# Attention and a feed-forward block in one kernel: heads split over the two row halves, scores over two banks, and the last eight units in one list

## The chip, the cores and the metric

The kernel runs on one core of one Trainium2 chip. The metric is the device time of one execution in microseconds (us). The profile used here is one execution, taken by the hardware profiler. Its engines are PE (TensorE, matrix products; PEld is its weight loads), DVE (VectorE), ACT (ScalarE), POOL (GpSimd) and SP (SyncE, which only issues DMA transfers here).

## The reference

Inputs are q, k, v of 4 batches x 8 heads x 768 tokens x 64 channels, 8 memory keys and values for each batch and head, and a feed-forward block of width 512 to 2048 and back. Attention goes by chunks of 32 queries; each chunk sees the 8 memory rows, 16 tokens to the left, its own 32 and 8 to the right, 64 rows in all.

```python
for c in range(nc):
    ...
    k_full = np.concatenate([mem_k, k_ctx], axis=2)
    v_full = np.concatenate([mem_v, v_ctx], axis=2)
    scores = scale * np.matmul(q_c, k_full.transpose(0, 1, 3, 2))
    scores = scores - np.max(scores, axis=-1, keepdims=True)
    a = np.exp(scores)
    a = a / (np.sum(a, axis=-1, keepdims=True) + 1e-09)
    out[:, :, c_start:c_end] = np.matmul(a, v_full)
...
xn = (x - mu) / np.sqrt(var + 1e-06) * g_ln
ch = np.maximum(xn @ w_ch1, 0.0) @ w_ch2
return (x + ch).astype(np.float32)
```

## The kernel before, in words

**Tiles and units.** The 3072 tokens are 24 tiles t of 128 tokens, six to a batch; t and t+1 form a unit u of 256 tokens, so there are 12 units. A tile passes through these steps:

- `qk_products` (line 311): 32 products of 32 queries x 64 keys, scores of 8 heads and 4 chunks, into one PSUM bank.
- `row_max`, `less_max` on DVE, `weights` (exp) on ACT, `pt_products` (four transposes on PE) and `pt_copy`.
- `val_products` (line 366): 32 products of 32 queries x 65 columns (64 channels and a column of ones that sums the weights) into the two banks of `two`.
- `tokens` on DVE divides by the sums and takes the mean, `shift` (ACT or POOL) subtracts it, `square` and `root_of` make the reciprocal deviation, `x_products` and `x_copy` turn the tile for the feed-forward block.

A unit then has eight `up_products` (two blocks of 128 hidden channels each, eight products of 128x256), each followed by `relu_up`, and seven `down7_products` of eight products each, the seven-product scheme of a 2x2 block product, with sums `r_sum` on DVE before and `add_to` on DVE behind. Units 10 and 11 go up in the seven-product scheme as well (`up7_products`, `hold`, `relu_of_sum`, `relu_sum`), whose weight sums are `w1_sum` and `x_sum`.

**Where operands lie.** Keys and queries are loaded as rows of 8 tokens (`load_octets`), interleaved by a copy (`mix`), turned by PE (`turn_whole`, called by `later_k` and `later_q`) and copied to KT (`to_stream`) and QD (`to_rows`). Of a pair of heads j, the even head lies on partitions 0 to 63 and the odd one on 64 to 127. The values lie in V: for each group of two chunks, chunk 0 of all heads on partitions 0 to 63 and chunk 1 on 64 to 127, with memory rows copied in by `v_mem` and the rows that both chunks see copied by `v_shared` (SBUF to SBUF, issued by SP). `load_v_head` and `load_v_ends` load V for batches 2 and 3.

**Positions in the array.** A product names its place by `tile_position`, a row half (0 or 64) and a column quarter (0, 32, 64, 96). Scores before use (0, 0), (64, 32), (0, 64), (64, 96), values the same four.

**PSUM.** Eight banks of 128x512: `one` (two, lent out in turn by `slot()`), `two` (two banks, for values), `upb` (two) and `dnb` (two).

**What sets the order.** Scheduling is manual: each engine runs its instructions in the order of the text, and waits on semaphores where data or banks are missing. Units 0 to 2 and 8 to 11 are written out call by call. Units 3 to 7 come from a plan: for each unit, 16 steps alternate `up` and `down7` of the unit before, and `at(u, step, ...)` places the rest. In it `val` of a tile and `qk` of the tile two later stand at one step, values first. A DMA issued by SP or POOL stands in that engine's queue like any other instruction.

Of the kernel before, what the change touches and what calls it, by code (L numbers as in the profile page):

```python
# [9 lines left out]
FP32 = mybir.dt.float32  # L10
# [8 lines left out]
def kernel(  # L19
# [33 lines left out]
    last = sb.tile([128, 1], FP16, name="last")  # L53
    w1c = [sb.tile([128, 4, 512], FP16, name=f"w1c{i}") for i in range(4)]
# [26 lines left out]
    one = [ps.tile([128, 512], FP32, name=f"one{i}") for i in range(2)]  # L81
# [29 lines left out]

    def load_v_head(b, h, part):

        base = (b * H + h) * HS
        if part == 0:
            nc.gpsimd.dma_start(  # L116
                out=V[b % 2][72:128, 0 : NG - 1, h, 0:64],
                in_=dram(v, base + 16 * D, [[64, 56], [64 * 64, NG - 1], [1, 64]]),
            )
        else:  # L120
            nc.gpsimd.dma_start(
                out=V[b % 2][0:32, 1:NG, h, 0:64],
                in_=dram(v, base + 48 * D, [[64, 32], [64 * 64, NG - 1], [1, 64]]),
            )

    def load_v_ends(b):
        nc.gpsimd.dma_start(
            out=V[b % 2][72:120, NG - 1, :, 0:64],
            in_=dram(v, b * H * HS + (64 * (NG - 1) + 16) * D, [[64, 48], [HS, H], [1, 64]]),
        )  # L130
        nc.gpsimd.dma_start(
            out=V[b % 2][16:32, 0, :, 0:64],
            in_=dram(v, b * H * HS, [[64, 16], [HS, H], [1, 64]]),
        )
# [131 lines left out]
    def mix(i, half, engine):  # L266
        for jj in range(2):
            mix_into(mixed[i], raw[i][half], jj, 96, engine)
# [41 lines left out]

    def qk_products(t, p=None):
        b, tt = t // 6, t % 6
        p = slot() if p is None else p
# [16 lines left out]
    def row_max(t, scores):  # L330
        nc.vector.tensor_reduce(out=nmx[t % 2], in_=scores, axis=AX.X, op=ALU.max)

    def less_max(t, scores):
        nc.vector.tensor_tensor(  # L334
            out=sub[t % 2].rearrange("p (c k) -> p c k", c=8), in0=scores,
            in1=free(nmx[t % 2], 0, [[1, 8], [0, 64]]), op=ALU.subtract,
        )
# [28 lines left out]
    def val_products(t):  # L366
        b, tt = t // 6, t % 6
        for h in range(H):
# [670 lines left out]
    mix(0, 0, "P")  # L1039
# [52 lines left out]

    plan = {}
# [6 lines left out]
    for u in range(3, NP - 4):  # L1100
# [12 lines left out]
    for b in range(2, B):  # L1113
        u0 = 3 * b - 3
        for half in range(2):
            w = u0 - 1 + half
            if w > 2:
                at(w, 1, load_octets, 0, half, k, b, 48 * half, 48)
                at(w, 3, load_octets, 1, half, q, b, 48 * half, 48)
                at(w, 12, mix, 0, half, "V")  # L1120
            at(w + 1, 5, mix, 1, half, "A")
            for n, step in enumerate((1, 6, 11, 15)):
                if n < 2:
                    at(w + 1, step, later_k, b, half, n, "V")
                else:
                    at(w + 1, step, later_q, b, half, n - 2, "A")
            for n in range(8):
                if w > 2:
                    step = (0, 2, 4, 12, 13, 14, 15, 16)[n]
                    at(w, step, load_v_head, b, 4 * half + n // 2, n % 2)  # L1130
                else:
                    at(4, n // 2, load_v_head, b, n // 2, n % 2)
        at(u0 + 1, 0, load_v_ends, b)
        at(u0 + 1, 10 if b == 2 else 6, v_shared, b, 0, NG)
        if b == 2:
            at(3, 8, v_mem, b)
        else:
            at(u0 + 1, 6, v_mem, b)
        at(u0, 14, mem_cols, KT[b % 2], memT[:, 4 * b : 4 * b + 4, :])
        at(u0, 14, mem_ends, KT[b % 2], memT[:, 4 * b : 4 * b + 4, :])  # L1140

    for u in range(2, NP - 5):
        for m, step in ((0, 0), (1, 1), (2, 3), (3, 5)):
            plan.setdefault((u + 1, step), []).insert(0, (r_sum, (u, m)))

    for u in range(3, NP - 4):
# [9 lines left out]

    r_sum(7, 0)
    up_products(8, 3, one[1])
    relu_up(8, 3, one[1], "A")
    val_products(18)  # L1160
    tokens(18)
    r_sum(7, 1)
    s20 = qk_products(20, upb[0])
    row_max(20, s20)
    up_products(8, 1, upb[1])
    w1_sum(2, 0, 1, "P")
    relu_up(8, 1, upb[1], "A")
    square(18)
    root_of(18)
    w1_sum(2, 0, 0, "P")  # L1170
    down7_products(7, 0, dnb[0])
    w1_sum(0, 0, 1, "P")
    down7_products(7, 1, dnb[1])
    add_to(14, 0, dnb[0])
    val_products(19)
    s21 = qk_products(21, one[0])
    less_max(20, s20)
    shift(18, "A")
    s22 = qk_products(22, one[1])
    w1_sum(0, 1, 1, "P")  # L1180
    up_products(8, 4, upb[1])
    w1_sum(0, 0, 0, "V")
    row_max(22, s22)
    weights(20)
    less_max(22, s22)
    weights(22)
    down7_products(7, 2, dnb[0])
    row_max(21, s21)
    add_to(14, 0, dnb[1])
    less_max(21, s21)  # L1190
    tokens(19)
    up_products(8, 0, upb[0])
    up_products(8, 5, one[1])
    relu_up(8, 4, upb[1], "A")
    relu_up(8, 5, one[1], "A")
    p20 = pt_products(20, dnb[1])
    pt_copy(20, p20, "A")
    x18 = x_products(18, upb[1])
    weights(21)
    r_sum(7, 2)  # L1200
    shift(19, "P")
    up_products(8, 6, one[0])
    down7_products(7, 3, one[1])
    square(19)
    p21 = pt_products(21, dnb[1])
    add_to(14, 1, dnb[0])
    add_to(15, 1, one[1])
    relu_up(8, 0, upb[0], "A")
    pt_copy(21, p21, "A")
    val_products(20)  # L1210
    tokens(20)
    relu_up(8, 6, one[0], "A")
    w1_sum(2, 1, 0, "P")
    down7_products(7, 4, dnb[0])
    add_to(15, 1, dnb[0])
    up_products(8, 7, upb[0])
    val_products(21)
    s23 = qk_products(23, dnb[1])
    r_sum(7, 3)
    x_copy(18, x18, "A")  # L1220
    tokens(21)
    relu_up(8, 7, upb[0], "A")
    up_products(8, 2, one[0])
    down7_products(7, 6, dnb[0])
    row_max(23, s23)
    less_max(23, s23)
    x19 = x_products(19, upb[1])
    relu_up(8, 2, one[0], "A")
    r_sum(8, 2)
    x_copy(19, x19, "A")  # L1230
    weights(23)
    shift(20, "P")
    r_sum(8, 0)
    down7_products(8, 1, upb[0])
    add_to(15, 0, dnb[0])
    w1_sum(1, 0, 0, "P")
    w1_sum(3, 0, 0, "P")
    shift(21, "P")
    down7_products(8, 0, one[0])
    add_to(16, 0, one[0])  # L1240
    r_sum(8, 1)
    p22 = pt_products(22, dnb[1])
    pt_copy(22, p22, "A")
    x21 = x_products(21, upb[1])
    down7_products(7, 5, one[1])
    val_products(22)
    x_copy(21, x21, "A")
    root_of(19)
    up_products(9, 3, dnb[0])
    relu_up(9, 3, dnb[0], "A")  # L1250
    up_products(9, 0, dnb[1])
    w1_sum(1, 0, 1, "P")
    square(20)
    square(21)
    w1_sum(0, 1, 0, "V")
    add_to(14, 1, one[1])
    store(14)
    tokens(22)
    shift(22, "P")
    p23 = pt_products(23, upb[1])  # L1260
    pt_copy(23, p23, "V")
    down7_products(8, 2, one[0])
    add_to(16, 0, upb[0])
    x20 = x_products(20, one[1])
    x_copy(20, x20, "A")
    add_to(16, 1, one[0])
    val_products(23)
    tokens(23)
    down7_products(8, 3, dnb[0])
    add_to(17, 1, dnb[0])  # L1270
    shift(23, "P")
    down7_products(8, 4, one[0])
    up_products(9, 2, upb[1])
    x22 = x_products(22, upb[0])
    add_to(17, 1, one[0])
    down7_products(8, 6, one[0])
    w1_sum(1, 1, 1, "V")
    x_copy(22, x22, "V")
    w1_sum(3, 1, 1, "P")
    x23 = x_products(23, one[1])  # L1280
    x_copy(23, x23, "V")
    x_sum(0, "V")
    x_sum(1, "P")
    x_sum(3, "P")
    relu_up(9, 0, dnb[1], "A")
    up_products(9, 1, dnb[1])
    up_products(9, 4, upb[0])
    relu_up(9, 4, upb[0], "A")
    w1_sum(3, 0, 1, "P")
    relu_up(9, 1, dnb[1], "A")  # L1290
    add_to(17, 0, one[0])
    store(17)
    up7_products(0, 1, one[1], False)
    r_sum(8, 3)
    hold(one[1], held[0][0])
    up_products(9, 7, one[0])
    relu_up(9, 7, one[0], "V")
    up7_products(0, 2, upb[0], False)
    up7_products(1, 1, dnb[1], False)
    hold(dnb[1], held[1][0])  # L1300
    down7_products(8, 5, dnb[0])
    add_to(16, 1, dnb[0])
    up_products(9, 6, one[0])
    relu_of_sum(0, 0, 0, upb[0], held[0][0])
    up7_products(0, 6, one[1], True)
    hold(one[1], held[0][1])
    up7_products(1, 6, dnb[1], True)
    hold(dnb[1], held[1][1])
    up7_products(1, 2, dnb[0], False)
# [160 lines left out]
```

## Time and profile before

| what | us |
|---|---|
| median of 3 runs (lowest, highest) | 224.51 (224.37, 224.60) |
| the profiled execution | 224.37 |
| its span, first to last instruction on the core | 222.7 |
| ACT busy | 132.8 |
| POOL busy | 133.9 |
| relu of the up products, ACT, one of 128x512 | 0.60 |
| add of a down product, DVE, one of 128x256 | 0.48 |
| transpose of a batch's keys or queries on PE, start to start | 0.345 |

The span leaves out 1.7 us around the first and last instruction. In a timeline a row gives start, duration, engine, line, operation, operands (written <- read) and how many were merged. A product's duration is its way through the array (0.27 us for 256 columns); products overlap, so what one costs is the distance between starts. In the answers by windows a row gives the stretch, its length, then busy time and count for each engine, the granted clock as a share of full speed, the busy share of the 16 DMA engines and GB/s. The granted clock is 1.0 in the whole span.

### The profile page before, as it was taken

The page shows a single profiled execution, that of the slowest core. Times are in us where ns is not written, and L with a number is a line of the kernel's source. Part 1 is how long each engine was busy: PE and PEld are TensorE (multiplying, and loading weights), DVE is VectorE, ACT ScalarE, POOL GpSimd, SP SyncE. Part 2 cuts the span into 40 slices and gives each one's busy share as a digit, 9 for nine tenths or more (in the row PEclk, how much of TensorE's full clock was granted, in tenths as well). Part 3 has the DMA queues.
Part 4 walks back from the last instruction along what each step waited for, and adds up shares of the span by engine and source line. Part 5 has one row for each costly group of instructions (what it writes and reads, how often), then busy time and mean ns, then how long its engine had stood idle before and what let it go on. Part 6 is the DMA issues. An engine that isn't in the chain of part 4 may idle for free.

```text
span 222.7 us, 8325 instructions
## 1 busy us (share of the span) xinstructions
PE 213.0 (96%) x3581; PEld 187.1 (84%) x3581; DVE 175.6 (79%) x388; ACT 132.8 (60%) x262; POOL 133.9 (60%) x210
## 2 busy tenths in 40 slices
PE   6986999999899999999999999999999999999993
PEld 2455877789888989999999999999898999999982
DVE  1587767888889887896686996995789987788983
ACT  3298875886775388468447278378757743654100
POOL 7948399989879617966454937415277548830000
PEclk9999999999999999999999999999999999999999
DMA  5999999999979993994952992952100011101115
GB/s 75 192 199 203 214 211 208 138 165 121 125 96 96 201 115 63 133 70 113 165 66 60 142 130 60 106 99 63 50 3 3 6 45 50 47 4 47 49 57 183
DMA packets 43450, 23.24 MB, mean 104 GB/s; under 512 B 30004, under 2 KB 39796, under 8 KB 43364
## 3 DMA queue, kind: packets, MB, share of 16 engines
q0 software_dynamic: 38416, 14.48, 56.8%
q1 hardware_dynamic: 4996, 8.22, 12.8%
q8 instruction: 28, 0.46, 0.9%
q14 instruction: 10, 0.08, 0.1%
HBM read 29.02 MB, written 6.29 MB: 159 GB/s over the span
## 4 chain that ended last, share of the span: by engine, by line
PE 78%; DMA 12%; POOL 6%; DVE 1%; issue 1%; ACT 0%; SPq 0%; POOLq 0%
PE dnb L643 21%; PE upb L464 20%; DMA w1c<-in_moe_w_ch_dram 6%; PE one L643 5%; PE upb L643 4%; PE one L464 4%; DMA V<-memv 3%; PE two L373 3%; DMA raw<-in_q_dram 3%; PE dnb L464 3%; PE one L274 3%; PE dnb L578 2%; POOL raw L107 2%; PE one L578 2%; PE one L322 2%; PE upb L490 2%
## 5 line engine op out<-in xcount | busy, mean ns | idle before, releaser
L464 PEld LDWEIGHTS <-w1c 128*128 128x128 f16 x640 | 67.2, 114 | 2.1 <-issue 0.5
L464 PE MATMUL upb<-xT,w1c 128*128 128x256 f16 x456 | 59.2, 273 | 0.3 <-ACT rT L456 0.3
L456 ACT ACTIVATE rT<-upb 128x512 f16<-128x512 f32 x55 | 32.1, 599 | 16.8 <-PE upb L464 16.6
L650 DVE SCALAR_TENSOR_TENSOR xs<-dnb,rstd,xs 128x256 f32<-128x256 f32 x55 | 26.4, 480 | 11.1 <-PE dnb L643 10.4
L643 PEld LDWEIGHTS <-RS 128*128 128x128 f16 x320 | 30.4, 98 | 3.2
L344 ACT ACTIVATE P<-sub 128x512 f16<-128x512 f32 x24 | 15.1, 632 | 22.7 <-DVE sub L334 22.7
L416 POOL TENSOR_SCALAR veps<-ssq 128x1 f32<-128x1 f32 x24 | 5.8, 240 | 34.4 <-ACT sq L409 33.5
L643 PEld LDWEIGHTS <-rT 128*128 128x128 f16 x240 | 23.0, 98 | 2.3
L643 PE MATMUL dnb<-T,RS 128*128 128x256 f16 x184 | 23.9, 273 | 0.0
L396 POOL TENSOR_SCALAR xn<-xs,nmean 128x512 f16<-128x512 f32 x17 | 12.5, 737 | 17.3 <-DVE nmean L389 13.0
L637 DVE TENSOR_TENSOR RS<-rT 128x1024 f16<-128x1024 f16 x18 | 13.5, 754 | 5.5 <-ACT rT L456 5.4
L409 ACT ACTIVATE sq<-xs,nmean 128x512 f16<-128x512 f32 x24 | 17.3, 722 | 0.2
L383 DVE CUSTOM_DVE_ANT_1 xs<-two,rec 128x512 f32<-128x512 f32 x24 | 16.6, 692 | 0.8
L643 PE MATMUL dnb<-w2c,rT 128*128 128x256 f16 x120 | 15.4, 272 | 0.0
L420 POOL TENSOR_TENSOR rstd<-veps,mhalf 128x1 f32<-128x1 f32 x24 | 13.8, 576 | 2.0
L116 POOL DMA_DIRECT2D V<-in_v_dram x16 | 13.4, 840 | 0.8 <-PE dnb L643 0.7
L464 PE MATMUL one<-xT,w1c 128*128 128x256 f16 x96 | 12.5, 273 | 0.2 <-DMA w1c<-in_moe_w_ch_dram 0.2
L241 DVE COPY KT<-one 128x192 f16<-128x192 f16 (+1 forms) x20 | 10.2, 550 | 3.2 <-PE one L228 2.6
L373 PEld LDWEIGHTS <-PT 64*32 64x32 f16 x768 | 7.4, 93 | 4.9 <-issue 3.3
L464 PE MATMUL dnb<-xT,w1c 128*128 128x256 f16 x88 | 11.3, 273 | 0.0
L274 PEld LDWEIGHTS <-raw 96*128 96x128 f16 x192 | 10.3, 98 | 0.9 <-issue 0.4
L373 PE MATMUL two<-V,PT 64*32 64x65 f16 x768 | 10.4, 191 | 0.6 <-DMA V<-memv 0.6
(197 smaller groups left out, 480.7 us busy)
## 6 DMA issues: line engine op xcount, KB each, us to landing
out_dram<-xs SPq DMA_DIRECT2D x23, 256.0 KB, 2.4
raw<-in_k_dram POOLq DMA_DIRECT2D x16, 192.0 KB, 5.6
raw<-in_q_dram POOLq DMA_DIRECT2D x12, 192.0 KB, 6.2
w1c<-in_moe_w_ch_dram POOLq DMA_DIRECT2D x4, 512.0 KB, 11.8
w2c<-in_moe_w_ch_dram POOLq DMA_DIRECT2D x4, 512.0 KB, 14.0
V<-in_v_dram POOLq DMA_DIRECT2D x16, 77.0 KB, 3.6
raw<-in_v_dram POOLq DMA_DIRECT2D x4, 192.0 KB, 6.8
V<-memv SPq DMA_DIRECT2D x6, 120.0 KB
```

The costliest lines, as they stand in the source:

```text
L116: nc.gpsimd.dma_start(out=V[b % 2][72:128, 0 : NG - 1, h, 0:64], in_=dram(v, base + 16 * D, [[64, 56], [64 * 64, NG - 1], [1, 64]]),)
L274: nc.tensor.matmul(out=pv[:, rows * r : rows * r + rows], lhsT=m[0:rows, jj, r, :], rhs=identity[0:rows, 0:rows], is_transpose=True, start ...
L344: nc.scalar.activation(out=P[t % 3], in_=sub[t % 2], func=ACTF.Exp, scale=0.125)
L373: nc.tensor.matmul(out=two[col : col + 32, 128 * h : 128 * h + 65], lhsT=PT[t % 3][rows, 2 * (h // 4) + h % 2, q0 : q0 + 32], rhs=V[b % 2] ...
L383: nc.vector.tensor_tensor_reduce(out=x.rearrange("p (h d) -> p h d", h=H), in0=free(two, 0, [[128, 8], [1, 64]]), in1=free(r, 0, [[1, 8], ...
L409: nc.scalar.activation(out=sq, in_=xs[t % 9], func=ACTF.Square, bias=nmean[t % 6], scale=1.0, accum_out=ssq[i],)
L420: nc.gpsimd.tensor_tensor(out=rstd[t % 9], in0=veps[i], in1=mhalf, op=ALU.pow)
L456: nc.scalar.activation(out=o, in_=i, func=ACTF.Relu)
L464: nc.tensor.matmul(out=p[:, 256 * hb : 256 * hb + 256], lhsT=free(w1c[hc // 4][:, dt, :], hc % 4, [[4, 128]]), rhs=xT[u % 3][:, dt, :], st ...
L637: nc.vector.tensor_tensor(out=R[k][:, lo:hi, :], in0=a[:, lo:hi, :], in1=b[:, lo:hi, :], op=op)
L643: nc.tensor.matmul(out=p[:, 0:256], lhsT=left[:, n, :], rhs=right(n), start=(n == 0 and not add), stop=(n == 7), skip_group_check=add,)
L650: nc.vector.scalar_tensor_tensor(out=x, in0=p[:, 0:256], scalar=rstd[t % 9], in1=x, op0=ALU.mult, op1=ALU.add,)
```

## The change

**Batches 2 and 3: other positions.** For tiles 12 to 23 heads 0 to 3 lie on partitions 0 to 63 and heads 4 to 7 on 64 to 127. `mix` pairs head f with head f+4, `memK` holds the memory keys in this order (`mem_halves`, four SBUF copies), and V is seen as `VC`: 24 chunks of four heads on each half. `load_v_ends` becomes four loads for two, `v_mem_chunks` four copies for two, `v_shared_chunks` two for one, and `v_edges` sets zeros and ones at the first and last chunks (four memsets and a copy on POOL). Each product of scores or values now has one of eight positions, a column quarter for each of four chunks and a row half for each half of the heads:

```diff
+    def qk_chunks(b, tt, p):
+        for j in range(4):
+            for c in range(4):
+                g = 2 * tt + c // 2
+                q0, k0 = 64 * g + 32 * (c % 2), BLK * g + 32 * (c % 2)
+                for x in range(2):
+                    rows, at = slice(64 * x, 64 * x + 64), 512 * x + 64 * j
+                    nc.tensor.matmul(
+                        out=p[32 * c : 32 * c + 32, at : at + 64],
+                        lhsT=QD[b % 2][rows, j, q0 : q0 + 32],
+                        rhs=KT[b % 2][rows, j, k0 : k0 + 64],
+                        start=True, stop=True, tile_position=(64 * x, 32 * c),
+                    )
+        return free(p, 0, [[64, 4], [512, 2], [1, 64]])
...
     def val_products(t):
         b, tt = t // 6, t % 6
+        if b >= 2:
+            for f in range(4):
+                for c in range(4):
+                    for x in range(2):
+                        rows, at = slice(64 * x, 64 * x + 64), 128 * (4 * x + f)
+                        nc.tensor.matmul(
+                            out=two[32 * c : 32 * c + 32, at : at + 65],
+                            lhsT=PT[t % 3][rows, f, 32 * c : 32 * c + 32],
+                            rhs=VC[b % 2][rows, 4 * tt + c, f, 0:65],
+                            start=True, stop=True, tile_position=(64 * x, 32 * c),
+                        )
+            return
...
+    def v_shared_chunks(b):
+        vc = VC[b % 2]
+        for lo in (0, 64):
+            nc.sync.dma_start(
+                out=vc[lo + 40 : lo + 64, 0 : 2 * NG : 2, :, :],
+                in_=vc[lo + 8 : lo + 32, 1 : 2 * NG : 2, :, :],
+            )
```

The scores of the upper heads go to one bank, those of the lower heads to another; values likewise, to the two banks of `two`.

**PSUM.** Up to the end of unit 3 the banks are as before. Then the two banks of `one` become `both`, one tile of 128x1024 that only scores use, from tile 12 to tile 23; transposes, turning, up and down products share the four banks of `upb` and `dnb`. After the scores of tile 23 are read, the two banks are `one` again.

**The order.** The plan covers unit 3 alone. Units 4 to 11 are one list, call by call, in which values and scores of different tiles stand apart. It begins so (with `...` where calls are left out):

```diff
+    phase.close()
+    phase = ExitStack()
+    psb = phase.enter_context(tc.tile_pool(name="psb", bufs=1, space=bass.MemoryType.PSUM))
+    both = psb.tile([128, 1024], FP32, name="both")
+
+    v_edges(2)
+    val_products(10)
+    load_v_head(2, 0, 0)
+    lk210 = turn_whole(mixed[0], 0, 96, upb[1])
+    load_octets(0, 0, k, 3, 0, 48, (1,))
+    s12 = qk_products(12, both)
+    row_max(12, s12)
...
+    up_products(4, 7, dnb[0])
+    relu_up(4, 7, dnb[0], "A")
+    up_products(4, 2, dnb[1])
+    relu_up(4, 2, dnb[1], "A")
...
+    mix(1, 0, "P", 3)
+    v_mem_chunks(2)
+    relu_up(5, 5, upb[0], "A")
+    down7_products(4, 4, upb[1])
+    add_to(9, 1, dnb[1])
+    add_to(9, 1, upb[1])
+    to_stream(KT[1], lk300, 0, "A", 48, 0)
+    v_shared_chunks(2)
+    val_products(12)
+    lq300 = turn_whole(mixed[1], 0, 96, upb[0])
+    s16 = qk_products(16, both)
+    row_max(16, s16)
+    down7_products(4, 5, dnb[1])
```

Which engine does a step changes in places with the list: three of batch 3's mixes are on POOL, several shifts on ACT, some copies on DVE. The steps of units 8 to 11 are the same as before in another order and with other banks.

## The prediction

> **What bounds the kernel now.** I read the page's shares and slices first, then TensorE's (PE's) timeline by start times from 83 us to the end, then counts in narrow windows, then SP's and ACT's timelines around the places that the change moves.
>
> ```profile
> PE 213.0 (96%) x3581; PEld 187.1 (84%) x3581; DVE 175.6 (79%) x388; ACT 132.8 (60%) x262; POOL 133.9 (60%) x210
> ...
> PE   6986999999899999999999999999999999999993
> ```
>
> PE is busy in nearly every slice. Busy is not yet full, so I looked at the pitch from start to start: eight products of 128x256 follow each other every 0.87 us, that is 109 ns each, and from 89.4 us (where unit 4 begins) to the last product at 218.0 us this pitch is kept almost everywhere. The chip therefore finishes when PE's list is through: a change pays only by what it takes from PE's list, and costs whatever PE then waits. The only places where PE loses time in that stretch are around the small attention products (the columns are start, duration, engine, line, operands, count):
>
> ```profile
> 108.99 1.04 PE L643 MATMUL dnb<-w2c,rT 128*128 128x256 f16 x8
> 109.96 0.42 PE L373 MATMUL two<-V,PT 64*32 64x65 f16 x32
> 110.22 0.44 PE L322 MATMUL one<-KT,QD 64*32 64x64 f16 x32
> 110.59 1.07 PE L464 MATMUL upb<-xT,w1c 128*128 128x256 f16 x8
> 111.49 1.04 PE L643 MATMUL dnb<-T,RS 128*128 128x256 f16 x8
> ...
> 160.20 0.42 PE L373 MATMUL two<-V,PT 64*32 64x65 f16 x32
> 160.45 0.69 PE L322 MATMUL one<-KT,QD 64*32 64x64 f16 x64
> 161.08 1.06 PE L464 MATMUL upb<-xT,w1c 128*128 128x256 f16 x8
> ...
> 166.79 0.39 PE L353 MATMUL dnb<-identity,P 128*128 128x128 f16 x4
> 167.11 0.42 PE L373 MATMUL two<-V,PT 64*32 64x65 f16 x32
> 167.47 1.05 PE L643 MATMUL dnb<-T,RS 128*128 128x256 f16 x8
> ```
>
> **Prices from these lines.** Going in: 109.96 - 108.99 is 0.97, 0.09 over the pitch of 0.87 (the four transposes from 166.79 show the same: 0.32 instead of 0.22). Values directly followed by scores: 110.59 - 109.96 = 0.63, and the next group starts 0.03 late (111.49 - 110.59 = 0.90). So a pair costs 0.09 + 0.63 + 0.03 = 0.75. Values alone: 0.09 + (167.47 - 167.11 = 0.36) = 0.45. A second set of scores behind the first adds 0.63 - 0.37 = 0.26. The way in and the way out of the small tiles are thus about half of each price.
>
> **Part one, values and scores apart.** For tiles 10 to 23 the trace has ten value-score pairs (10 x 0.75), one value with two scores (0.09 + 0.88 + 0.03 = 1.00) and three values alone (3 x 0.45): 9.85 us for 14 values and 12 scores. Read down the new list, no value stands next to a score on PE any more; each of the 26 groups pays its own way in and out. At the price of a group alone that is 26 x 0.45 = 11.7 us, 1.85 us more.
>
> **Part two, eight tiles in place of four.** Before, 32 products of a set go to four positions (two row halves, but each column quarter with one half only). After, each of four column quarters is used with both halves, so eight positions. A group's 32 products start over 0.236 us (eight rounds of about 29 ns: four starts within 10 ns, then a pause until the 64 columns have passed). If eight ran at once, four rounds would do: 0.12 us less per group, 0.33 instead of 0.45. That bounds it from below: 2 x 0.45 (tiles 10 and 11 keep the old form) + 24 x 0.33 = 8.8 us, 1.0 us less than before. The other bound is no gain, 1.85 us more. Which end? The counts in narrow windows decide (scores' line; after the length come busy and count of products, then of weight loads):
>
> ```profile
> 64.90:65.00 0.10, 0.10 (x27) 0.10 (x28) 1.00 0.06 10
> ...
> 160.65:160.75 0.10, 0.10 (x36) 0.10 (x23) 1.00 0.00 0
> 160.75:160.85 0.10, 0.10 (x35) 0.10 (x23) 1.00 0.00 0
> ```
>
> A load's record lasts 0.09, so a window of 0.10 sees the loads that started in 0.19: 28 early in a stream (6.8 ns each), but 23 later (8.3 ns each). At 64.8 the scores came first and ran at the early rate, the values behind them at the late one; at 160.2 it is the other way round. So the late rate belongs to no kind of product: after some 40 to 50 pairs of load and product, PE's supply of instructions is at its end and gives one pair per 8.3 ns. Working back from where the rate changes, a stream starts with a lead of only 5 to 9 pairs. Eight positions can't run faster than that: (32 - 7) x 8.3 ns = 0.21 us in place of 0.236. I take 0.42 per group, near the upper bound: 0.90 + 24 x 0.42 = 11.0 us, **+1.1 us**.
>
> [...]
>
> **Part three, the list of units 4 to 11.** The same 48 up, 63 down, 28 seven-product up, 12 turning and 26 transposing groups stand in both orders: 119.3 us at their pitches (0.875, 0.875, 0.44, 0.345, 0.22), so nothing there. What can change is waiting. Before, PE loses 0.5 us from 89.4 us on (0.13 before 98.65, 136.3 and 197.5, 0.12 before 153.3). After: `both` takes the banks of `one`, and the first scores, s12, are third in the list. They need the last to_rows of unit 3:
>
> ```profile
> 89.72 0.79 ACT L249 COPY QD<-one 128x768 f16<-128x768 f16 x1
> ...
> 99.17 0.79 SPq L153 DMA_DIRECT2D V<-V  x1
> ...
> 130.00:147.00 17.00, 17.00 (x299) 15.68 (x297) 14.36 (x36) 11.20 (x21) 7.58 (x13) 1.00 0.73 98
> ```
>
> That ends at 90.51, while PE is through the values of tile 10 and one turning group at about 90.3: 0.2 us. Then up, down, transposes and turning share four banks where they had six. A bank is taken for 0.875, plus 0.17 until the last product ends, plus 0.48 (DVE's add) or 0.60 (ACT's relu), 1.6 us, and four banks in turn come round after 3.5 us, so 1.9 us of delay on DVE or ACT fits. DVE is the tight one: 14.36 of 17 us in the stretch shown, and 112 of some 131 us for the new list by its own rows. I walked the first 25 us by these durations and found arrivals in order, several by 0.1 to 0.3 us only. Taken: 0.2 + 0.7, less the 0.5 that goes, **+0.4 us** (bounds -0.5 and +4).
>
> **Part four, V, its copies and memory.** POOL issues the same 32 head loads, but eight end loads for four (4 x 0.58 = 2.3 us more) and two sets of edges (about 1.2 us each from the memsets of 0.62 us for 640 elements); three mixes of 2.07 us move to it from DVE and ACT. All of that is 70 us of POOL's work in 131, so it costs nothing unless a load is late. SP issues 8 memory copies for 4, 4 shared copies for 2 and 4 halves, at 0.75 to 0.79 each; before them SP has stores only, whose adds come earlier. The tight one is the shared copy of batch 2: it waits for the end loads, which POOL reaches some 12 us of work after its last unit-3 load (90.85), so issued by 104.8, landed at about 107.5; the copy before took 3.9 us from its issue at 99.17 to its last packet at 103.1. So about 112 to 113, and PE wants the values of tile 12 at about 113.4. Cover of about 1 us (before it had 7); if gone, every us late is a us of the end. Taken as 0.
>
> **The sum.** The profiled execution took 224.37 (span 222.7); 224.37 + 1.1 + 0.4 = 225.9. The median of the runs is 0.14 higher: **226.0 us**. The end (last product, one add, two stores) has the same form in both lists.
>
> **Rivals.** (a) Eight tiles do run at once: 24 x 0.33, so -1.0 + 0.4 = **223.9**. For it: four starts within 10 ns show that PE can issue a load and a product in 3.3 ns when it has them. Against it: the late rate. It decides from the point where the 32 products of a group start within 0.14 us, because then 24 groups fall below 8.55 us, what they had less the 0.4. This is the side of faster. (b) The copies of V come late for tile 12 (or 18): packets of 640 bytes in place of 15,360, on a DMA system at 0.73 in these stretches; a copy from memory values issued at 53.87 landed 7.2 us later. 2 us late gives **228.0**. Against it: the shared copy went through quickly before. (c) Four banks are too few: some 70 up and down groups of units 4 to 7, each 0.05 us late, give 3.5 us in place of the 0.7: **228.8**. For it DVE's load; against it the 1.9 us of room. (d) The change does nothing to the rate (four at once after all): +1.85 + 0.4 = 226.7, which lies in the forecast's own range.
>
> **How the numbers follow.** Forecast with (d) 0.55, own range 225.2 to 227.2; (a) 0.20; (b) 0.12; (c) 0.13. The range takes in most of (a) and (b) and half of (c): 223.7 to 228.3. Within 0.2% (0.45 us, about what a measurement can tell) means 224.1 to 225.0: the upper tail of (a) and the lower of the forecast, 0.12. Faster, from (a), 0.18; slower 0.70.
>
> **What would show it.** The new groups of 32 in PE's timeline: next start 0.32 to 0.33 after the first where I am right about supply, 0.24 if eight run at once. No groups next to each other. Before the values of tiles 12 and 18 no wait on a V copy; before s12 about 0.2. DVE's and ACT's idle before the add and relu lines stays, if the banks suffice. I am wrong if PE's waits after 90 us sum to over 2 us, or if its groups shrink below 0.36 with the way in.

## The result, and the profile after

The changed kernel takes 232.45 us (median of 6 runs, 230.55 to 233.10) beside 224.44 for the kernel before (6 runs): ratio 1.0337, interval 1.0286 to 1.0388. Forecast were 226.0 and a range up to 228.3. The direction was right, the size was not. Medians here and below are of all runs of a kernel, while a ratio leaves out the slow ones, over 1.5% above the fastest of their kernel.

The profiled execution took 230.55, its span is 228.8 where before had 222.7. Lines of the page, those that answer to the ones shown of before, and the group of `r_sum` (its mean in before: 754 ns):

```profile
PE 216.1 (94%) x3581; PEld 186.4 (81%) x3581; DVE 177.1 (77%) x381; ACT 135.9 (59%) x279; POOL 138.8 (61%) x225
...
PE   6997999999999999999679998999999999999992
...
PEclk9999999999999999999979999999999999999999
...
L731 DVE TENSOR_TENSOR RS<-rT 128x1024 f16<-128x1024 f16 x18 | 18.4, 1022 | 1.1 <-ACT rT L550 0.8
```

PE's busy time is only 3.1 us longer. The loss is mostly idle time, and two slices (5.72 us each) hold most of it: the second 6 in PE's row and the 7 behind it, 108.7 to 120.1 us, with a 7 in the clock's row under the second of them. The timelines of PE, POOL and DVE there:

```profile
111.48 1.04 PE L558 MATMUL upb<-xT,w1c 128*128 128x256 f16 x8
116.02 1.45 PE L737 MATMUL upb<-T,RS 128*128 128x256 f16 x8 [3.50 <-DVE xs L744]
117.40 0.42 PE L455 MATMUL two<-V,PT 64*32 64x65 f16 x32
```

```profile
110.20 0.58 POOL L111 DMA_DIRECT2D raw<-in_q_dram  x1
110.78 2.02 POOL L321 COPY raw<-raw 96x1024 f16<-96x1024 f16 x2
112.76 2.25 POOL L636 TENSOR_TENSOR raw<-w1c 128x512 f16<-128x512 f16 x2
114.97 0.60 POOL L111 DMA_DIRECT2D raw<-in_k_dram  x1
```

```profile
110.26 0.47 DVE L744 SCALAR_TENSOR_TENSOR xs<-dnb,rstd,xs 128x256 f32<-128x256 f32 x1
110.66 4.92 DVE L731 TENSOR_TENSOR RS<-rT 128x1024 f16<-128x1024 f16 x1
115.50 0.47 DVE L744 SCALAR_TENSOR_TENSOR xs<-upb,rstd,xs 128x256 f32<-128x256 f32 x1
```

Read from the end: PE's `down7_products(4, 4)` can have its bank only after `add_to(8, 1)`; that add stands on DVE behind `r_sum(4, 2)`; and this sum, 0.68 us at most other places, takes 4.92. It ends 0.57 us after the last of four POOL instructions in a row that read SBUF: the two copies of `mix(1, 0, "P", 3)` and `w1_sum(0, 0, 0)`, `w1_sum(0, 1, 0)`. DVE's other work beside POOL's copies, the adds and `row_max` with one operand in PSUM, keeps its durations (an add of 128x256 takes 0.47 to 0.49 us and `row_max` 0.68 to 0.69 everywhere in this trace). The same stands at two later places: `r_sum(5, 3)` takes 2.24 us beside `shift(14)` and `w1_sum(0, 1, 1)`, and `r_sum(6, 0)` 2.21 beside `w1_sum(3, 1, 0)`; PE waits 0.87 and 0.25 behind them. (These waits and the 3.66 below are read from start to start, less the pitch; the row's own figure for the long one, 3.50, is PE's idle time.)

What follows the long wait, by windows (stretch, length, busy time of PE, PEld, DVE, ACT, POOL, granted clock, DMA, GB/s):

```profile
112.00:116.00 4.00, 0.52 (x5) 0.35 (x4) 4.00 (x3) 1.35 (x3) 4.00 (x5) 1.00 0.51 76
116.00:120.00 4.00, 3.98 (x86) 2.76 (x86) 2.13 (x4) 0.80 (x1) 0.20 (x1) 0.57 0.59 65
```

The granted clock falls to 0.57, and products of 256 columns start 213 ns apart in place of 109 until about 119.9. That costs about 1.6 us more, which no wait shows.

The account of the 6.1 us between the spans: 3.7 (wait for the add) + 1.6 (clock) + 0.9 + 0.2 (the later sums) + 0.3 (s12, by starts) + 0.4 (the end, below) + 0.1 (211 us), less 0.5 that the small groups gave and 0.4 of waits that before had: 6.3, so nothing large is left to find in this execution. The median execution takes 1.9 us more than this one, at a mean granted clock of 0.985 over the span in place of 0.993. That clock alone would be some 1.8 us (an estimate: 0.008 of 230), as if the half clock described above had lasted about twice as long; no trace of such an execution shows it.

The groups are the side of the change that did what it says:

```profile
122.76 0.32 PE L455 MATMUL two<-V,PT 64*32 64x65 f16 x32
123.00 1.06 PE L558 MATMUL dnb<-xT,w1c 128*128 128x256 f16 x8
...
125.75 0.31 PE L374 MATMUL both<-KT,QD 64*32 64x64 f16 x32
125.99 0.40 PE L523 MATMUL upb<-identity,xn 128*128 128x128 f16 x4
```

The next product starts 0.24 us after the first of a group, in place of 0.36. How much of that comes from eight positions at once is asked by the last experiment.

### The profile page after: what moved, and what is told of

Read it like the earlier page. It is cut to its first block, busy times and chain, and to the rows that moved or that the text cites. A ratio compares the mean times of both kernels' runs of the same rounds, so it can differ in the third digit from the quotient of the medians.

```text
span 228.8 us, 8374 instructions
## 1 busy us (share of the span) xinstructions
PE 216.1 (94%) x3581; PEld 186.4 (81%) x3581; DVE 177.1 (77%) x381; ACT 135.9 (59%) x279; POOL 138.8 (61%) x225
## 4 chain that ended last, share of the span: by engine, by line
PE 82%; DVE 11%; ACT 2%; issue 2%; DMA 1%; SPq 0%; DVEq 0%; ACTq 0%
PE upb L558 13%; PE dnb L737 13%; PE upb L737 11%; PE dnb L558 10%; DVE RS L731 4%; PE last L737 3%; PE last L558 2%; PE one L558 2%; PE last L672 2%; PE dnb L672 2%; DVE xs L744 2%; PE upb L584 2%; PE dnb L330 2%; PE upb L330 2%; PE dnb L584 2%
## 5 line engine op out<-in xcount | busy, mean ns | idle before, releaser
L558 PE MATMUL upb<-xT,w1c 128*128 128x256 f16 x328 | 42.1, 273 | 0.3 <-ACT rT L550 0.3
L550 ACT ACTIVATE rT<-upb 128x512 f16<-128x512 f32 x39 | 23.0, 600 | 12.7 <-PE upb L558 10.9
L558 PE MATMUL dnb<-xT,w1c 128*128 128x256 f16 x216 | 28.0, 273 | 0.0
L744 DVE SCALAR_TENSOR_TENSOR xs<-dnb,rstd,xs 128x256 f32<-128x256 f32 x37 | 17.6, 478 | 8.3 <-PE dnb L737 8.1
L731 DVE TENSOR_TENSOR RS<-rT 128x1024 f16<-128x1024 f16 x18 | 18.4, 1022 | 1.1 <-ACT rT L550 0.8
L550 ACT ACTIVATE rT<-dnb 128x512 f16<-128x512 f32 x23 | 13.8, 602 | 8.2 <-PE dnb L558 7.9
L744 DVE SCALAR_TENSOR_TENSOR xs<-upb,rstd,xs 128x256 f32<-128x256 f32 x29 | 13.8, 479 | 5.2 <-PE upb L737 4.9
L737 PE MATMUL dnb<-T,RS 128*128 128x256 f16 x120 | 15.6, 273 | 0.1
L737 PE MATMUL upb<-T,RS 128*128 128x256 f16 x88 | 11.8, 279 | 3.5 <-DVE xs L744 3.5
L111 POOL DMA_DIRECT2D raw<-in_k_dram x16 | 9.9, 620 | 2.1 <-POOLq L1868 0.9
```

Source lines behind the costliest of these rows:

```text
L111: nc.gpsimd.dma_start(out=raw[i][half][par : 2 * n : 2], in_=dram(src, (b * H + par) * HS + 512 * lo, [[512, n], [2 * HS, 4], [1, 512]]),)
L550: nc.scalar.activation(out=o, in_=i, func=ACTF.Relu)
L558: nc.tensor.matmul(out=p[:, 256 * hb : 256 * hb + 256], lhsT=free(w1c[hc // 4][:, dt, :], hc % 4, [[4, 128]]), rhs=xT[u % 3][:, dt, :], st ...
L731: nc.vector.tensor_tensor(out=R[k][:, lo:hi, :], in0=a[:, lo:hi, :], in1=b[:, lo:hi, :], op=op)
L737: nc.tensor.matmul(out=p[:, 0:256], lhsT=left[:, n, :], rhs=right(n), start=(n == 0 and not add), stop=(n == 7), skip_group_check=add,)
L744: nc.vector.scalar_tensor_tensor(out=x, in0=p[:, 0:256], scalar=rstd[t % 9], in1=x, op0=ALU.mult, op1=ALU.add,)
```

## The experiments

Theory, read from the rows above: DVE sums with both inputs in SBUF stand still while POOL reads SBUF (4.92 us in place of 0.68); the clock (0.57) follows from PE's idle time (3.50 us). Rivals: V late at tile 12, the DMA traffic, or the four banks. Ratios are to the kernel before, run beside it on the same chip.

**The two weight sums later** (`e1_sums_later`).

```diff
-    w1_sum(0, 0, 0, "P")
...
-    w1_sum(0, 1, 0, "P")
...
     shift(12, "P")
+    w1_sum(0, 0, 0, "P")
+    w1_sum(0, 1, 0, "P")
```

> Port theory (a DVE sum of two SBUF tiles stands still while POOL reads SBUF, through all POOL instructions that follow each other): r_sum(4, 2), which took 4.92 us beside two copies and two weight sums, now stands beside the two copies alone and takes about 2.7 us (to 113.4). PE's wait of 3.66 us falls to about 1.5, the clock stays at full speed, and the kernel takes 226.5 to 228 us. Rival (the sum waits for its own input, or the four banks are too few, and POOL has nothing to do with it): r_sum(4, 2) still 4.9, kernel 230.5 to 232.5.

Measured 226.88 us, ratio 1.0151 (1.0087 to 1.0214). DVE's timeline, then PE's:

```profile
110.47 2.89 DVE L731 TENSOR_TENSOR RS<-rT 128x1024 f16<-128x1024 f16 x1
```

```profile
113.81 1.03 PE L737 MATMUL upb<-T,RS 128*128 128x256 f16 x8 [1.47 <-DVE xs L744]
```

Two of the four POOL readers gone takes 2.03 us from the sum (they last 2.25 together), PE waits 1.5, the clock stays at 1.00, and some 4 us of the loss (1.0337 to 1.0151) are gone by two lines that move 2.3 us of POOL's work.

**No POOL reads beside the sum** (`e2_no_pool_reads`): the same, and the mix on DVE.

```diff
-    mix(1, 0, "P", 3)
+    mix(1, 0, "V", 3)
```

> Port theory: with the mix of the queries on DVE (0.8 us) and the weight sums later, POOL reads nothing beside r_sum(4, 2) and r_sum(4, 3); both take 0.7 us, PE's wait there falls under 0.3, and the kernel takes 224.5 to 226 us (waits of 0.87 and 0.25 behind the other two slow sums stay). Rival (order or banks): the wait at this place stays over 2 us, kernel over 229.

Both `r_sum` take 0.68 us and the wait for the add is gone. The time hardly moves: 227.48, ratio 1.0119 (1.0058 to 1.0181). The profiled execution took 225.48, inside what was expected; the other three took 226.83 to 229.95. Its timeline of PE shows what still waits:

```profile
112.07 0.20 PE L455 MATMUL two<-V,PT 64*32 64x65 f16 x1
113.52 0.31 PE L455 MATMUL two<-V,PT 64*32 64x65 f16 x31 [1.25 <-DMA V<-V]
```

The values of tile 12 are reached, start, and stop after one product for the shared copies of V. This is the prediction's rival (b); the stall of DVE had hidden it. That the same wait is longer in the other three is likely, but no trace shows it.

**POOL as busy, but only writing** (`e3_pool_writes`): the mix and both sums, which are left out, replaced by four memsets in the same places.

```diff
-    mix(1, 0, "P", 3)
+    nc.gpsimd.memset(mixed[1][0:96, 0], 0.0)
+    nc.gpsimd.memset(mixed[1][0:96, 1], 0.0)
...
-    w1_sum(0, 0, 0, "P")
+    nc.gpsimd.memset(raw[0][0].rearrange("p j r d -> p (j r d)")[:, 0:1024], 0.0)
...
-    w1_sum(0, 1, 0, "P")
+    nc.gpsimd.memset(raw[0][0].rearrange("p j r d -> p (j r d)")[:, 1024:2048], 0.0)
```

> POOL is as long busy beside r_sum(4, 2) as in the changed kernel, but with memsets, which write SBUF and read nothing; the mix of a quarter of batch 3's queries and two weight sums are left out. If only POOL's reads block: r_sum(4, 2) 0.7 us, kernel 224.5 to 226. If any POOL access to SBUF blocks: r_sum(4, 2) 4 to 5 us, kernel 230 to 232.5.

DVE and POOL:

```profile
110.43 1.49 DVE L731 TENSOR_TENSOR RS<-rT 128x1024 f16<-128x1024 f16 x1
...
112.23 0.68 DVE L731 TENSOR_TENSOR RS<-rT,RS 128x1024 f16<-128x1024 f16 x1
```

```profile
109.36 2.01 POOL L321 COPY raw<-raw 96x1024 f16<-96x1024 f16 x2
111.32 0.58 POOL L111 DMA_DIRECT2D raw<-in_q_dram  x1
111.89 0.97 POOL L1357 MEMSET raw<- 96x1024 f16 x1
112.78 0.97 POOL L1358 MEMSET raw<- 96x1024 f16 x1
```

`r_sum(4, 2)` is held by the tail of the earlier `mix(0, 0)` copies, to 0.55 us after them; `r_sum(4, 3)`, wholly beside memsets, takes its 0.68. So here it is POOL's reads that hold the sum, not POOL's being busy. (POOL's DMA issues do not hold it either: in e2 the sum that takes 0.68 us from 109.40 stands beside two of them.) 227.54 us, ratio 1.0131 (1.0082 to 1.0180): V is late here as well (waits of 0.77 and 1.17 at the values of tile 12).

**PE kept at work in the wait** (`e4_pe_kept_warm`).

```diff
+    warm(12, upb[0])
     down7_products(4, 4, upb[1])
```

> Twelve products of zeros (2.6 us) into a free bank fill PE's wait before down7 (4, 4); the wait itself stays. If the slow products behind the wait (213 ns in place of 109) come from PE's idle time: all products behind it take 109 ns, the granted clock is 1.0, and the kernel takes 228.9 to 229.3 (230.55 less about 1.6). If the slow clock has another cause (load, heat): it stays at 0.98 to 0.99 and the time at 230.5 to 232.5.

The stall is the same (`r_sum(4, 2)` 5.28 us, though here it starts 0.49 us ahead of POOL's copies), but the window after it reads otherwise. DVE and POOL, then the window:

```profile
110.46 5.28 DVE L731 TENSOR_TENSOR RS<-rT 128x1024 f16<-128x1024 f16 x1
```

```profile
110.95 2.02 POOL L321 COPY raw<-raw 96x1024 f16<-96x1024 f16 x2
112.93 2.26 POOL L636 TENSOR_TENSOR raw<-w1c 128x512 f16<-128x512 f16 x2
```

```profile
116.00:120.00 4.00, 3.81 (x100) 3.17 (x100) 3.10 (x8) 0.80 (x1) 0.37 (x1) 1.00 0.61 65
```

Clock 1.00, products 109 ns apart, and 229.28 us in four runs that lie within 0.9 us (ratio 1.0235, 1.0203 to 1.0266). Against the changed kernel's 1.0337 that is some 2 us; between the two profiled executions 1.35 (230.55 - 229.20). With PE kept at work the clock in this window is 1.00, without it 0.57: the half clock came from PE's idle time.

**V's copies earlier** (`e8_v_earlier`, on e2).

```diff
     load_v_head(2, 3, 0)
+    load_v_ends(2)
     load_v_head(2, 3, 1)
+    v_shared_chunks(2)
...
-    load_v_ends(2)
...
-    v_shared_chunks(2)
```

> The kernel without POOL's reads beside r_sum(4, 2), with one more edit: the ends of batch 2's V are loaded 11 steps earlier and its two SBUF-to-SBUF copies are issued some 10 us earlier. Theory (the copies were late, rival b of the prediction, and the stall of VectorE had hidden it): the wait of val_products(12) for V, 1.25 us in that kernel's profile, goes, nothing comes in its place, a profile of about 224.3 us, a median of 225.0 to 226.5 against 227.5, and the runs lie closer together than 225.5 to 228.1. Rival (the wait is hidden behind something else, such as the PT copy of tile 12 or the softmax of tile 16): val_products(12) starts no earlier, median within 0.5 us of 227.5.

It missed: 229.39 us, ratio 1.0196 (1.0125 to 1.0266), slower if anything. PE's timeline, then SP's:

```profile
113.14 0.20 PE L455 MATMUL two<-V,PT 64*32 64x65 f16 x1
113.92 0.20 PE L455 MATMUL two<-V,PT 64*32 64x65 f16 x2 [0.58 <-DMA V<-memv]
115.16 0.20 PE L455 MATMUL two<-V,PT 64*32 64x65 f16 x1 [1.03 <-DMA V<-memv]
115.95 0.31 PE L455 MATMUL two<-V,PT 64*32 64x65 f16 x28 [0.60 <-DMA V<-in_v_dram]
```

```profile
100.58 1.89 SPq L161 DMA_DIRECT2D V<-V  x2
102.52 3.27 SPq L171 DMA_DIRECT2D V<-memv  x4
```

The shared copies are in time, and other pieces of V late. In the changed kernel SP issues the four memory copies from 89.1 us on; here they stand in its queue behind the shared copies, which wait for their loads until 100.58. The loads of V for chunk heads issued from 102 to 106 us take 10.7 us to land (median of four) in place of 4.1 in the changed kernel. What slows them is not shown: the DMA share from 100 to 110 us is no higher than in the changed kernel (0.93 and 1.28 for its two halves as the profile counts it, against 1.63 and 1.13), and besides the six copies the loads of batch 3's queries and keys, issued in the same 4 us, take longer too (7.0 us, where the one issued in that time in the changed kernel took 5.0).

**The later weight sums moved too** (`e5_all_moved`, on e8).

```diff
-    w1_sum(0, 1, 1, "P")
...
     load_v_head(3, 5, 0)
+    w1_sum(0, 1, 1, "P")
...
     w1_sum(1, 1, 0, "P")
+    w1_sum(3, 1, 0, "P")
...
-    w1_sum(3, 1, 0, "P")
```

> On top of the V loads and copies moved earlier: w1_sum(0, 1, 1) and w1_sum(3, 1, 0) on POOL moved to places where VectorE has no sum of two SBUF tiles. Port theory: r_sum(5, 3) and r_sum(6, 0) fall from 2.2 to 0.68 us each, PE's waits behind them of 0.86 and 0.23 us go, 1.0 us less than the kernel with the V copies moved; by the account (the groups of small products 0.55 shorter, s12 0.26 longer, the end 0.46 longer, 0.1 at 211 us, 0.38 of old waits gone) 223.8 to 225.0 us, where before has 223.9. Rival (VectorE has slack enough there; PE waits for something else): less than 0.4 us.

`r_sum(5, 3)` and `r_sum(6, 0)` fall to 1.12 and 0.95 us, and PE's waits behind them go. 227.96 us, ratio 1.0135 (1.0086 to 1.0185), about 1.4 us below e8, with intervals that overlap. The rest was not met, because V is still late (0.63 + 0.72 + 0.65 us) and the clock halves behind it (0.59 from 116 to 120 us).

**Stores earlier** (`e6_and_stores`, on e5).

```diff
     add_to(18, 1, one[0])
+    store(18)
...
     add_to(20, 1, one[0])
+    store(20)
...
-    store(18)
...
-    store(20)
```

> On top of all moved: store(18) and store(20) issued right after their last add. If the late stores make the end 0.46 us longer: 0.3 to 0.5 us less than the kernel without it, last add to end of 3.1 instead of 3.55 us. Rival (the last store alone sets the end): no change within 0.2 us.

Ratio 1.0136 (1.0081 to 1.0192), no difference. From PE's last product to the end it is 4.2 us in place of 4.3 (before 3.87): the place of these stores is not the cause.

**Four positions at a time** (`e7_four_at_once`, on e5): the products of rows 0 to 63 first, then those of rows 64 to 127.

```diff
-        for j in range(4):
+        for x, j in [(x, j) for x in range(2) for j in range(4)]:
             for c in range(4):
...
-                for x in range(2):
+                if True:
...
-            for f in range(4):
+            for x, f in [(x, f) for x in range(2) for f in range(4)]:
                 for c in range(4):
-                    for x in range(2):
+                    if True:
```

> On top of all moved (stores as they were): the small products of each group in another order, the 16 of rows 0 to 63 first and then the 16 of rows 64 to 127, so that only four of the eight positions are in use at a time. If eight at once is where the shorter groups come from: first to last start 0.236 us again instead of 0.125, 24 groups, 2.4 to 2.9 us longer than the kernel with all moved. Rival (the way in and out of a group, some 0.23 us of it, hides the second half): under 1 us.

Late V and the clock drown it: 1.0152 (1.0123 to 1.0181) beside 1.0135. The trace alone tells something: 0.160 to 0.168 us from first to last start where no clock disturbs it, neither the 0.125 of eight positions nor the 0.236 of before. It was asked again on a kernel without these waits.

**V in the order of need** (`e9_v_first`, on e5).

```diff
     v_edges(2)
+    v_mem_chunks(2)
...
     load_v_head(2, 1, 1)
+    load_v_head(2, 2, 1)
+    load_v_head(2, 0, 1)
...
-    load_v_head(2, 2, 1)
...
-    load_v_head(2, 0, 1)
...
-    v_mem_chunks(2)
```

> On top of all moved, the pieces of batch 2's V in the order that val_products(12) needs: the four copies of memv are issued on SP before the two V<-V copies (in the kernel with the V copies moved they stood behind them and were issued at 102.5 to 105.1 us instead of 89 to 93), and the two last part-1 loads come ahead of batch 3's queries on POOL's queue. Theory (what was left of the loss is V late at tile 12, and the half clock behind that wait): the three waits of 0.65 + 0.72 + 0.63 us and the products at 213 ns after them go, 223.5 to 225.0 us, ratio to before 0.998 to 1.004. Rival (the DMA engines are full from 95 to 115 us, so whichever transfer comes last is late, now the queries and keys of batch 3): a wait of 1 us or more comes out at lq300 or s16 or remains at val_products(12), 226 us or more.

224.72 us in 12 runs, ratio 1.0031 (1.0003 to 1.0060). PE from 112 to 116 us, and the only wait left from 85 us to the end:

```profile
112.00:116.00 4.00, 3.99 (x100) 3.19 (x99) 3.81 (x10) 2.15 (x4) 1.26 (x3) 1.00 0.95 122
```

```profile
PE both L374 <- ACT QD L299: 0.2, 1, 0.2
```

Of 7 to 8 us lost, all but 0.7 are back, by changes of place and one mix moved from POOL to DVE: no product, no bank, no position and no transfer differs from the changed kernel. So four banks are enough, and the DMA traffic is not too much in itself; its order was.

**V's order alone** (`e10_only_v_first`: the edits of V on the changed kernel, POOL's reads where the change put them).

> The changed kernel with the order of V's pieces alone mended, POOL's copies and sums where the change put them. If the stall of VectorE behind POOL's reads is the first cause and the late V stands hidden behind it: r_sum(4, 2) still 4 to 5 us, PE's wait for add_to(8, 1) still about 3.5 us, then half clock, and the median within 1.0 us of the changed kernel's 230.5 to 232.5. Rival (the late V is the main loss): 227 us or less.

228.57 us, 0.9 below the 229.5 that was the least expected, with runs from 225.12 to 230.61; the ratio, 1.0121 (1.0040 to 1.0203), rests on two of the four. DVE and PE in the profiled execution, the slowest of the four:

```profile
109.99 1.55 DVE L731 TENSOR_TENSOR RS<-rT 128x1024 f16<-128x1024 f16 x1
...
111.86 4.45 DVE L731 TENSOR_TENSOR RS<-rT,RS 128x1024 f16<-128x1024 f16 x1
```

```profile
116.76 1.86 PE L737 MATMUL dnb<-w2c,RS 128*128 128x256 f16 x8 [2.80 <-DVE xs L744]
```

```profile
116.00:120.00 4.00, 3.24 (x16) 2.35 (x17) 3.09 (x8) 0.00 (x0) 0.94 (x2) 0.50 0.55 60
```

The stall is there, now on `r_sum(4, 3)`, since POOL's copies wait for a load until 108.98 and come at another moment. So what the stall costs depends on which sum POOL meets. PE is idle for 2.80 us, less than in the changed kernel, yet here the clock stays at half for 6.8 us (115.7 to 122.5, by windows of 0.5 us) in place of 3.4 (116.5 to 119.9). PE works in 5.7 us of that, so about 2.9 us are lost (an estimate: half of 5.7) in place of 1.6. That the run of 225.12 us met no stall is a guess; no trace shows it.

**One store less** (`e11_one_store`, on e9).

```diff
-    store(23, 256, 512)
...
-    store(23, 0, 256)
+    store(23)
```

> The kernel with V first, with tile 23 stored by one transfer where two halves were. In the traces SP's stores and copies take eight semaphores in turn, and SP waits for them at the end in the order of their numbers, 0.06 us for each. In before the last store has the seventh of the eight (last landing 2.88 us after PE's last product, end 3.87); in the changed kernel, which issues more copies on SP, it has the first, and the other seven waits stand behind it (2.95, end 4.30). One transfer less gives the last store the eighth. Theory: the end comes 3.85 us after PE's last product, 0.4 us less, 224.2 to 224.5 beside 224.7. Rival (the landing itself is what came later): end 4.2 or more, no change.

From PE's last product to the end 4.08 us, 0.22 less where 0.45 was expected: the seven waits behind the last landing are gone, but it comes at 3.16 in place of 2.95; the one larger store that now precedes it may be why, which was not tried. 224.16 us in 12 runs; ratio 0.9998 (0.9971 to 1.0025). This is the changed kernel with its order mended (and one mix back on DVE, one store for two): level with before, not better.

**Four positions at a time, again** (`e12_four_at_once`): the edit of e7 on e11.

> The same with the small products ordered so that only four of the eight positions are in use at a time. Its first trial, beside late V, showed 0.160 to 0.168 us from first to last start in place of 0.123 to 0.128, not the 0.236 of before's order. If that holds and nothing else moves: 24 groups by 0.04, 0.9 to 1.0 us longer than the kernel with one store. Rival (part of a group's way in and out, 0.23 us, covers the second half): under 0.4 us.

225.14 us, ratio 1.0024 (1.0002 to 1.0046): 0.98 us over e11 by the medians, 0.6 by the ratios, whose intervals overlap. The same group of values in e11 and then in e12:

```profile
167.05 0.32 PE L455 MATMUL two<-V,PT 64*32 64x65 f16 x32
167.30 1.05 PE L737 MATMUL dnb<-T,RS 128*128 128x256 f16 x8
```

```profile
167.57 0.35 PE L455 MATMUL two<-V,PT 64*32 64x65 f16 x32
167.86 1.05 PE L737 MATMUL dnb<-T,RS 128*128 128x256 f16 x8
```

0.29 against 0.25 to the next start; over 24 groups the first-to-last times sum to 4.09 against 3.00 us, 1.09 more. The trace thus agrees with the expected 0.9 to 1.0 us, and that is what the use of both row halves at once is worth here. It is the smaller part of what a group gained: the first-to-last time fell from 0.236 us in before to 0.125, and with four positions at a time it is 0.17. The larger part comes with the new layout (heads by row halves, a bank for each half, the order of the products), whose pieces no run tells apart.

## Why the prediction was wrong

**Part four failed, and with it the forecast.** It asked of POOL's 70 us of work only whether a load would be late, and found that otherwise it "costs nothing". Where POOL reads SBUF beside an `r_sum`, DVE pays: 4.2 us at one place, 1.6 and 1.5 at two others, and PE 4.8 in all. The hint stood in the trace of before, where a group of `r_sum` has a mean of 754 ns, though most of them take 680:

```profile
L637 DVE TENSOR_TENSOR RS<-rT 128x1024 f16<-128x1024 f16 x18 | 13.5, 754 | 5.5 <-ACT rT L456 5.4
```

The long sums of before (five, of 1.10 to 1.65 us) all lie beside a `w1_sum`, an `x_sum` or a `shift` on POOL.

Beside memsets, which write and read nothing, the sum took its 0.68 us (e3). Who began first did not decide who waited: in the changed kernel the sum began at 110.66 us, 0.12 ahead of POOL's first copy at 110.78, and waited for four POOL instructions that began after it, and so did the sum of e4, which began 0.49 us ahead of the first.

**The clock was no term of the sum.** A wait was priced at its length. PE's wait of 3.50 us cost 1.35 to 1.6 us more in the profiled executions. The length of one wait does not tell when the clock halves: 2.80 us were enough in e10 (0.50 from 116 to 120 us), and in e5 three waits of 0.63 to 0.72 us with a few products between them (0.59).

**Cover of V, "about 1 us".** There was none: once nothing else held PE, the shared copies of batch 2 were 1.25 us late. The step that failed is the end loads, "issued by 104.8, landed at about 107.5". SP's timeline of the changed kernel has the copies they release:

```profile
107.81 2.17 SPq L161 DMA_DIRECT2D V<-V  x2
```

The end load that the second copy reads was issued at 105.88 and landed 3.3 us later; that copy went out at 109.19, and such a copy took 4.9 us (108.61 to 113.52 in e2) where 3.9 was assumed, so about 114.1 against PE's want at 113.4. This is rival (b), but as a second cause: in the changed kernel PE came at 117.4, and no wait on V is to be seen.

**Part two, 0.42 us per group.** Measured are 0.36 (0.09 in, 0.24 to the next start, 0.03), so parts one and two together give 0.90 + 24 x 0.36 = 9.5 us against 9.85: a gain of 0.3 (0.5 when read group by group in both traces) in place of the loss of 1.1. The step that failed is the supply of one pair per 8.3 ns with a lead of 5 to 9 pairs: 32 products start in 0.123 us, 3.9 ns each. The late rate read in before was not a limit of supply. Whether two row halves lose time by sharing a bank is open: 0.236 us with a shared bank, 0.17 and 0.125 with a bank for each half, where positions and order differ as well. Rival (a)'s point of decision (0.14 us) was reached, but its gain of 0.6 us is not shown for the whole kernel: the mended kernel has a ratio of 0.9998 (0.9971 to 1.0025), though its time of 224.16 us is near the 223.9.

**Right** were the wait of s12 (0.2 forecast, 0.19 measured), that four banks suffice (in e9 no wait for a bank is left, so the 0.7 of small waits was too much), and that no two groups stand next to each other.

**The end** does not have "the same form": 0.43 us more, and not from any transfer. SP's stores and copies take eight semaphores in turn, and at the end SP waits for them by number, 0.06 us each. The copies that the change adds shift the turn, so that the last store has the first number, with seven waits behind its landing (SP passes the first wait at 227.42 us, the seven others follow up to 227.85); in before it had the seventh, with one wait behind it (221.69, then 221.75).

## What to carry to other kernels

Before a step moves to POOL, list what DVE does at that moment: here a sum of two SBUF tiles waited out a whole row of four POOL reads (4.92 us in place of 0.68), while adds from PSUM kept their 0.47 to 0.49. Price a wait of PE not by its length alone but by the clock behind it, which here cost 1.6 us in one execution and about 2.9 in another. And when a stall goes and the time does not, look at what stands right behind it: here V's shared copies were late behind DVE's stall and hidden by it. And when a transfer moves forward in a queue, look at what it now holds up: bringing the shared copies forward made V's memory copies late.

## What the runs showed of the hardware that was not expected

- A DVE sum can wait through a chain of POOL reads: 4.92 us for four, 2.89 for two, 1.49 for the tail of one, each ending 0.55 to 0.57 us after POOL's last. It does not always wait for the whole chain. In the changed kernel the `r_sum` at 167.85 us took 0.99: it ended 0.55 us after a `shift`, and the `w1_sum` behind that `shift` took 1.58 in place of 1.17. In before the sums at 169.05 and 184.69 went in between two POOL instructions in the same way. What decides is open.
- The half clock: none after single waits of 1.25 and 1.47 us (e2, e1); yes after one of 2.80 in e10, two that sum to 1.9 in e3, three that sum to 2.0 in e5 and 2.2 in e8; none after three that sum to 2.2 in e6. It lasted 3.4 us in the changed kernel and 6.8 in e10. What decides is open.
- Four positions at a time start 32 products in 0.160 to 0.168 us when a row half is done whole, in 0.236 in before's order, where row halves alternate and share a bank. Which of the two makes the difference was not tried.
